# Forward attention segments in two head halves, with the token rows projected beside the memory rows

## The chip, the cores and the metric

One NeuronCore of one Trainium2 chip runs the whole program in one launch. The metric is device time in microseconds, the median of several executions. A single execution of each kernel is also recorded by the hardware profiler; the views of the profile quoted here come from that execution.

## The reference, cut to what matters

The function is a transformer block, forward and all its gradients. A sequence of 2048 rows of 448 is normalised, sent through a recurrent attention, added to the input, normalised again and sent through a gated FFN (1792 wide), and added once more. The recurrence is what sets the order of the work:

```python
for s in range(n_seg):                       # 64 segments of 32 rows
    h = concatenate([mem, xs], axis=1)       # 8 memory rows + 32 rows = 40
    q, k, v = h @ Wq, h @ Wk, h @ Wv         # 16 heads of 256
    scores = where(mask, q @ k.T * scale, -1e9)
    o = (softmax(scores) @ v) @ Wo
    mem = o[:, :M]                           # the next segment needs these 8 rows
    outs.append(o[:, M:])
```

The outputs are the block's result and the gradients of the input, the first memory and the seven weights, ten arrays in all.

## The kernel before, in words

The program has four stages: `forward_chain`, `ffn_phase` (FFN forward and backward), `backward_chain` and `tail_phase` (weight gradients from what the other stages stored). A tile is 128 rows, four segments; there are 16 tiles. A block is 16 segments.

**One forward segment.** The 40 rows of a segment stand as columns of `hT_roll`, the 32 rows first and the 8 memory rows after them. Heads are held in pairs (g = 0 on partitions 0 to 39, g = 1 on partitions 64 to 103). The steps, in order: `wpass` for Q and for K (L427, 128 matmuls of 40 columns each, evicted by DVE at L75 or ACT at L76); the scores of all heads into one PSUM tile (L486); the value rows, four PSUM tiles of two 512-column halves each (L494); the softmax on DVE and ACT over 128x320 (scale and mask L500, maximum L504, subtract L505, exp L506, sum L510, reciprocal L512, product L513); P turned by matmuls with the identity (L517) and copied into `PT_bd`, one half by DVE and one by ACT; the heads' outputs (L525); their memory columns copied to `o8`, which L535 multiplies with Wo: 32 matmuls of 8 rows, spread over four groups of 32 partitions of `pO`. The four groups are summed by copying them to fp32 (`om`, L541 and L542) and multiplying with a stack of four identities (L545), which also turns the result, and L548 casts that into `hT_roll` for the next segment. The 32 token columns of each head output go to `xblk`, and after every fourth segment L564 multiplies the whole tile with Wo (32 matmuls of 448 columns into `fx`); DVE adds the input rows (L565), the sum goes to `Hh` in memory, and its statistics are taken (L568, L569).

**Order.** Within `k.prio.crit()` instructions have a priority of their own, so they keep their order and stand ahead of everything else; what lies outside, such as L564, is put by the scheduler into places where TensorE would wait. Each engine then runs its own list strictly in order. SyncE (SP) issues the hardware queue's transfers and all transposing ones, GpSimd (POOL) the software queue's; both lists are in order too, and an issue waits there for its data. PSUM tiles for the chain come from one ring of five.

**Stores.** Every segment stores Q and P (POOL, L551 and L553) and K and V (SP, L552 and L554), and copies its memory rows on POOL (L555, L556). At the end of a tile `xblk` is turned by transposing DMA (L437) and stored to `X_o` (L439); at the end of a block `mblk`, the memory rows of the 16 segments, too. Weights are turned piece by piece through the same two staging buffers (L463, L464).

**FFN and tail.** In the last segment `_FFNLoads.at` asks for the FFN's weights at four places. The FFN needs the standard deviation of every tile: two square roots on ACT (L658), for tiles 0 to 11 and for the rest. `backward_chain` ends with the layer norm's gradient of tile 0: `DH` is fetched in two halves through one buffer (L983), and the result stored (L987). `tail_phase` begins with the gradient of Wo: `X_o`, 16 tiles of tokens and 4 of memory rows, is loaded on SP (L1031); the matching rows of `DHb` are loaded into `DCt` by four transfers on POOL (L1059); and L1095 sums over the 20 blocks, tokens first, six PSUM tiles at a time, 0.187 us a matmul.

Of the kernel before, what the change touches and what calls it, by code (L numbers as in the profile page):

```python
# [15 lines left out]
P = 128  # L16
# [129 lines left out]
def run_all(k: _K):  # L146
# [43 lines left out]
    nc.gpsimd.affine_select(out=mask1[:], in_=mask1[:], compare_op=ALU.is_ge, fill=-1e9,  # L190
# [13 lines left out]
    def dt(name, shape, dtype=BF16):  # L204
# [8 lines left out]
              X_o=dt("X_o", [NB, P, MC * P]), HC=dt("HC", [NB * P, DP]))  # L213
# [93 lines left out]
def forward_chain(k: _K):  # L307
# [13 lines left out]
    Wo_sb = W(96, MC, D)  # L321
    qT_b = [A(4 * i, 32, 64) for i in range(2)]
# [9 lines left out]
    mh = B(7.25, KC, P)  # L332
    PT_bd = B(0.25, 8, 2, L)
    o8_b = [B(1.5 + 0.5 * i, 32, M) for i in range(2)]
    x2_b = [B(2.5 + 0.875 * i, D) for i in range(2)]
    P_b = [B(4.25 + 0.625 * i, 8, L) for i in range(2)]
    h_b = [B(5.5 + 0.875 * i, D) for i in range(2)]
# [7 lines left out]
    om = k.f32("f1", DP, "om")  # L345
    nc.gpsimd.memset(om[:], 0.0)
    pO = k.po1()
    nc.vector.memset(pO[:], 0.0)

# [70 lines left out]
    def wpass(W_sb, s, dst):  # L420
        sl = s % NWIN
        pss = [k.ps1() for _ in range(3)]
        for j in range(MC):
            c = cj(j)
            b, jj = divmod(j, 12)
            for kc in range(KC):
                nc.tensor.matmul(pss[b][:, jj * L:(jj + 1) * L], lhsT=W_sb[:, kc, c * P:(c + 1) * P], rhs=hT_roll[:, kc, sl, :],  # L427
                                 start=(kc == 0), stop=(kc == KC - 1))
        for b in range(3):
            n = min(12, MC - 12 * b)  # L430
            k.evac(dst[:, 12 * b:12 * b + n, 0:L], pss[b][:, 0:n * L].rearrange("p (c n) -> p c n", n=L), "vsv"[b])
# [33 lines left out]

    for s in range(NSEG):
# [3 lines left out]
        qT, kT, Vs, o8, P_sb = qT_b[s % 2], kT_b[s % 2], V_b[s % 2], o8_b[s % 2], P_b[s % 2]  # L470
        xblk, x_t2, h_t = xblk_b[t % 2], x2_b[t % 2], h_b[t % 2]
        if r == 0:
            nc.gpsimd.dma_start(out=x_t2, in_=X2[t * P:(t + 1) * P, :])
        with k.prio.crit():
            wpass(Wq_sb, s, qT)
            if s == NSEG - 1:
                k.fl.at(0)
            wpass(Wk_sb, s, kT)
            if s == NSEG - 1:
                k.fl.at(1)  # L480
            pS = k.ps1()
            for h in range(8):
                for g in range(2):
                    for dc in range(DC):
                        j = 2 * (2 * h + dc) + g
                        nc.tensor.matmul(pS[64 * g:64 * g + 64, h * L:(h + 1) * L], lhsT=qT[:, j, :], rhs=kT[:, j, 0:L],  # L486
                                         start=(dc == 0), stop=(dc == DC - 1), skip_group_check=True)

            pV = [k.ps1() for _ in range(4)]
            for b in range(4):  # L490
                for kc in range(KC):
                    for g in range(2):
                        n = 4 * g + b
                        nc.tensor.matmul(pV[b][64 * g:64 * g + 64, 0:512], lhsT=hT_flat[:, kc, sl * L:sl * L + 64],  # L494
                                         rhs=Wv_sb[:, kc, n * 512:(n + 1) * 512],
                                         start=(kc == 0), stop=(kc == KC - 1), skip_group_check=True)
            if s == NSEG - 1:
                k.fl.at(2)
            S_sb = k.f32("f2", 8 * L, "S_sb")[:].rearrange("p (h n) -> p h n", n=L)
            nc.vector.scalar_tensor_tensor(  # L500
                out=S_sb, in0=pS[:, 0:8 * L].rearrange("p (h n) -> p h n", n=L), scalar=k.scale,
                in1=maskb[:].unsqueeze(1).to_broadcast([P, 8, L]), op0=ALU.mult, op1=ALU.add)
            mx = smal.tile([P, 8], FP32, name="mx")
            nc.vector.tensor_reduce(out=mx[:], in_=S_sb, axis=AX.X, op=ALU.max)  # L504
            nc.vector.tensor_tensor(out=S_sb, in0=S_sb, in1=mx[:].unsqueeze(2).to_broadcast([P, 8, L]), op=ALU.subtract)  # L505
            nc.scalar.activation(out=S_sb, in_=S_sb, func=ACT.Exp)  # L506
            for b in range(4):
                k.evac(Vs[:, b * 512:(b + 1) * 512], pV[b][:, 0:512], "s")
            ssum = smal.tile([P, 8], FP32, name="ssum")
            nc.vector.tensor_reduce(out=ssum[:], in_=S_sb, axis=AX.X, op=ALU.add)  # L510
            rs = smal.tile([P, 8], FP32, name="rs")
            nc.vector.reciprocal(out=rs[:], in_=ssum[:])  # L512
            nc.vector.tensor_tensor(out=P_sb, in0=S_sb, in1=rs[:].unsqueeze(2).to_broadcast([P, 8, L]), op=ALU.mult)  # L513
            pPT = k.ps1()
            for h in range(8):
                for g in range(2):
                    nc.tensor.matmul(pPT[64 * g:64 * g + L, h * L:(h + 1) * L], lhsT=P_sb[:, h, :],  # L517
                                     rhs=ident[:, 64 * g:64 * g + L], start=True, stop=True, skip_group_check=True)
            for g in range(2):
                k.evac(PT_bd[64 * g:64 * g + L, :, g, :],  # L520
                       pPT[64 * g:64 * g + L, 0:8 * L].rearrange("p (h n) -> p h n", n=L), "vs"[g])
            pso = [k.ps1() for _ in range(3)]
            for cl in range(16):
                b, i = divmod(cl, 6)
                nc.tensor.matmul(pso[b][:, i * 2 * L:(i + 1) * 2 * L], lhsT=Vs[:, cl * P:(cl + 1) * P],  # L525
                                 rhs=PT_bd[:, cl // 2, :, :].rearrange("p g n -> p (g n)"), start=True, stop=True)
            ov = []
            for b in range(3):
                n = min(12, 32 - 12 * b)
                v = pso[b][:, 0:n * L].rearrange("p (c n) -> p c n", n=L)  # L530
                ov.append((12 * b, n, v))
                k.evac(o8[:, 12 * b:12 * b + n, :], v[:, :, SEG:L], "vsv"[b])
            if s + 1 < NSEG:
                for j in range(MC):
                    nc.tensor.matmul(pO[32 * (j % 4):32 * (j % 4) + M, 0:D], lhsT=o8[:, j, :], rhs=Wo_sb[:, cj(j), :],  # L535
                                     start=(j < 4), stop=(j >= MC - 4), skip_group_check=True)
            for (c0, n, v) in ov:
                k.last_x = getattr(k, "last_x", {})
                k.last_x["svs"[c0 // 12]] = k.evac(xblk[:, c0:c0 + n, r * SEG:(r + 1) * SEG], v[:, :, 0:SEG], "svs"[c0 // 12])
# [9 lines left out]
        if s == 0:  # L549
            stats(2, NT, to_h.ins)  # L550
# [31 lines left out]
def ffn_phase(k: _K, back):  # L582
# [73 lines left out]
    for t0, t1_ in ((0, NT - 4), (NT - 4, NT)):  # L656
        with tc.issue_after(k.last_x["s"].ins):
            nc.scalar.activation(out=sd[:, t0:t1_], in_=mv2[:, t0:t1_, 1], func=ACT.Sqrt, bias=k.eps_t[:], scale=1.0)  # L658
        with tc.issue_after(k.last_x["v"].ins):
            nc.vector.reciprocal(out=rstd2[:, t0:t1_], in_=sd[:, t0:t1_])  # L660
# [552 lines left out]
```

## Time and profile before

| | us |
|---|---|
| median of 4 runs | 3345.87 |
| lowest and highest | 3337.11, 3356.5 |
| the profiled execution, time | 3337.11 |
| the profiled execution, span | 3335.3 |
| TensorE busy | 3035.5 (91%) |
| DVE busy | 1310.8 (39%) |
| ACT busy | 974.2 (29%) |
| POOL busy | 645.3 (19%) |
| mean granted TensorE clock | 0.972 |

The span runs from the first to the last instruction of the profiled execution; 1.8 us of its time lie around it. PE in the views is TensorE; PEld is its weight loading, which runs beside the matmuls. In the chain of waits a line is a start, a length and what was at work: it follows the end of the program back from instruction to instruction to whatever released each one. In a line of a group, the numbers behind the bar are busy time in us, the mean of one instruction in ns (for a matmul it includes the time in which the next ones already stream, so it is longer than the distance between two), and the idle time just before, with what ended it.

### The profile page before, as it was taken

What the parts mean: (1) busy time and instruction counts of PE and PEld (TensorE: products, weight loads), DVE (VectorE), ACT (ScalarE), POOL (GpSimd) and SP (SyncE); (2) the same over time, 40 slices, a digit from 0 to 9 for tenths busy, and PEclk for the clock granted to TensorE, in tenths of its full rate; (3) what the DMA queues carried; (4) which work ended last, traced back from release to release, by engine and by line L of the source; (5) the groups of instructions that cost most, each with busy time, mean ns of one, the idle gap of its engine ahead of it and who ended that gap; (6) DMA issues with size and microseconds to landing.
All of it is one profiled execution on the core that took longest, in us unless ns stands there. A gap on an engine that the chain in (4) does not pass through costs nothing.

```text
span 3335.3 us, 121108 instructions
## 1 busy us (share of the span) xinstructions
PE 3035.5 (91%) x55076; PEld 2054.6 (62%) x55086; DVE 1310.8 (39%) x2919; ACT 974.2 (29%) x2178; POOL 645.3 (19%) x1344
## 2 busy tenths in 40 slices
PE   5899999999999969995998999999999899999998
PEld 3676777777777746663666666666666544444443
DVE  4434444444344347773444444444454301111110
ACT  2323323333233223332333333333333201120110
POOL 3111211111111121221121111222222212112111
PEclk8999999999999989997999999999999999999999
DMA  7756865656675498888777788887878997969952
GB/s 262 196 152 168 214 180 162 188 162 182 183 197 162 135 288 192 202 197 274 151 167 167 156 168 163 169 167 165 174 166 174 271 277 209 198 177 198 198 148 70
DMA packets 993208, 619.57 MB, mean 186 GB/s; under 512 B 897476, under 2 KB 907796, under 8 KB 990196
## 3 DMA queue, kind: packets, MB, share of 16 engines
q1 hardware_dynamic: 921428, 361.57, 52.1%
q0 software_dynamic: 71264, 250.24, 22.1%
q8 instruction: 431, 7.06, 0.9%
q14 instruction: 85, 0.70, 0.1%
HBM read 123.54 MB, written 269.69 MB: 118 GB/s over the span
## 4 chain that ended last, share of the span: by engine, by line
PE 70%; DVE 9%; issue 9%; DMA 7%; ACT 2%; POOL 1%; SPq 1%; ACTq 0%; DVEq 0%; POOLq 0%
PE psf L427 12%; PE psf L1074 8%; PE po L903 7%; PE psf L494 5%; PE psf L860 5%; PE psf L837 4%; PE po L535 3%; PE psf L1095 3%; PE fx L564 3%; PE fx L962 3%; PE fx L731 2%; PE psf L650 2%; PE fx L1079 2%; DVE arA L75 2%; PE psf L925 2%
## 5 line engine op out<-in xcount | busy, mean ns | idle before, releaser
L76 ACT CAST arA<-psf 128x320 bf16<-128x320 f32 (+4 forms) x1139 | 487.3, 447 | 1537.2 <-PE psf L427 450.7
L75 DVE CAST arA<-psf 128x384 bf16<-128x384 f32 (+6 forms) x1029 | 492.5, 496 | 1014.5 <-PE psf L427 330.1
L427 PE MATMUL psf<-arA,arW 128*128 128x40 bf16 x16384 | 436.7, 181 | 38.6 <-issue 18.1
L427 PEld LDWEIGHTS <-arW 128*128 128x128 bf16 x16384 | 433.2, 97 | 55.2 <-issue 33.3
L903 PE MATMUL po<-arW,arA 128*32 128x448 bf16 x6144 | 358.5, 364 | 48.2 <-DVE arA L75 44.3
L494 PE MATMUL psf<-arW,arA 128*64 128x512 bf16 x2048 | 260.6, 383 | 3.6 <-DMA arW<-in_A_Wv_dram 3.6
L1074 PE MATMUL psf<-arW,arA 128*128 128x512 bf16 x1030 | 259.5, 379 | 0.0
L903 PEld LDWEIGHTS <-arA 128*32 128x32 bf16 x6144 | 154.8, 98 | 166.6 <-DVE arA L75 47.3
L1074 PEld LDWEIGHTS <-arA 128*128 128x128 bf16 x1440 | 136.0, 98 | 164.8 <-issue 13.8
L860 PEld LDWEIGHTS <-arW 128*128 128x128 bf16 x8192 | 213.0, 96 | 29.5 <-issue 29.5
L860 PE MATMUL psf<-arA,arW 128*128 128x40 bf16 x8192 | 217.0, 179 | 10.3 <-DVE arA L929 5.1
L650 PE MATMUL psf<-arW 128*128 128x256 bf16 x1344 | 156.4, 276 | 40.9 <-DMA arW<-arW 29.6
L494 PEld LDWEIGHTS <-arA 128*64 128x64 bf16 x2048 | 147.8, 111 | 71.1 <-DMA arW<-in_A_Wv_dram 4.6
L650 PEld LDWEIGHTS <-arW 128*128 128x128 bf16 x1344 | 132.9, 99 | 66.6 <-issue 33.7
L75 DVE CAST arB<-psf 40x320 bf16<-40x320 f32 x320 | 107.9, 337 | 99.9 <-PE psf L525 66.1
L837 PEld LDWEIGHTS <-arW 128*128 128x128 bf16 x2048 | 88.0, 101 | 67.9 <-issue 64.9
L76 ACT CAST arB<-psf 128x96 bf16<-128x96 f32 (+1 forms) x320 | 98.1, 307 | 105.4 <-DVE arB L75 52.8
L564 PE MATMUL fx<-arW,arA 128*128 128x448 bf16 x512 | 124.5, 353 | 0.6 <-ACT arA L76 0.6
L870 ACT COPY arA<-psf 128x1024 bf16<-128x1024 bf16 x128 | 123.3, 1015 | 5.9 <-PE psf L869 4.4
L535 PE MATMUL po<-arW,arB 128*8 128x448 bf16 x2016 | 110.7, 363 | 9.6 <-DMA arW<-in_A_Wo_dram 5.9
L837 PE MATMUL psf<-arB,arW 128*128 128x80 bf16 x2048 | 98.9, 203 | 18.9 <-DVE arB L887 7.1
L1095 PEld LDWEIGHTS <-arW 128*128 128x128 bf16 x606 | 58.9, 99 | 72.5 <-DMA arW<-X_o 13.0
(259 smaller groups left out, 3808.5 us busy)
## 6 DMA issues: line engine op xcount, KB each, us to landing
QT<-arA POOLq DMA_DIRECT2D x64, 512.0 KB, 4.9
KT<-arA SPq DMA_DIRECT2D x64, 512.0 KB, 3.6
VG<-arA SPq DMA_DIRECT2D x64, 512.0 KB, 3.8
X_o<-arA POOLq DMA_DIRECT2D x40, 512.0 KB, 4.4
X_v<-arA POOLq DMA_DIRECT2D x32, 512.0 KB, 6.7
X_k<-arA POOLq DMA_DIRECT2D x32, 512.0 KB, 4.0
X_q<-arA POOLq DMA_DIRECT2D x32, 512.0 KB, 4.2
arW<-X_o SPq DMA_DIRECT2D x30, 512.0 KB, 11.5
```

What stands on the lines that cost most here:

```text
L75: return nc.vector.tensor_copy(out=out, in_=in_)
L76: return nc.scalar.copy(out=out, in_=in_)
L427: nc.tensor.matmul(pss[b][:, jj * L:(jj + 1) * L], lhsT=W_sb[:, kc, c * P:(c + 1) * P], rhs=hT_roll[:, kc, sl, :], start=(kc == 0), stop=( ...
L494: nc.tensor.matmul(pV[b][64 * g:64 * g + 64, 0:512], lhsT=hT_flat[:, kc, sl * L:sl * L + 64], rhs=Wv_sb[:, kc, n * 512:(n + 1) * 512], sta ...
L535: nc.tensor.matmul(pO[32 * (j % 4):32 * (j % 4) + M, 0:D], lhsT=o8[:, j, :], rhs=Wo_sb[:, cj(j), :], start=(j < 4), stop=(j >= MC - 4), sk ...
L564: nc.tensor.matmul(px[:, 0:D], lhsT=xblk[:, j, :], rhs=Wo_sb[:, cj(j), :], start=(j == 0), stop=(j == MC - 1))
L650: nc.tensor.matmul(ps[:, f2 * 256:(f2 + 1) * 256], lhsT=Wt[:, kc, c * P:(c + 1) * P], rhs=xT[:, kc, :], start=(kc == 0), stop=(kc == KC - 1))
L837: nc.tensor.matmul(ps[b][:, i * 2 * L:(i + 1) * 2 * L], lhsT=lhs[:, cl, :], rhs=rhs_bd[:, cl // 2, :, :].rearrange("p g n -> p (g n)"), st ...
L860: nc.tensor.matmul(pss[b][:, jj * L:(jj + 1) * L], lhsT=WoT_sb[:, kc, c * P:(c + 1) * P], rhs=do_roll[:, kc, sl, :], start=(kc == 0), stop ...
L903: nc.tensor.matmul(pH[32 * (j % 4):32 * (j % 4) + 32, 0:D], lhsT=blk[nm][:, j, r * SEG:(r + 1) * SEG], rhs=WT[:, cj(j), :], start=(nm == " ...
L1074: nc.tensor.matmul(pa[2 * kc + g][:, 0:w], lhsT=lhs_of(b)[:, kc * P:(kc + 1) * P], rhs=rhs_of(b, g), start=(b == 0), stop=(b == nblk - 1), ...
L1095: nc.tensor.matmul(pa[i][:, 0:D], lhsT=lhs_of(b, i), rhs=rhs_of(b), start=(bi == 0), stop=(bi == len(nblk) - 1))
```

## The change

In the forward chain the 16 heads of a segment are handled in two halves of 8 (four pairs). Q, K, scores, softmax, transposes and head outputs are made for half 0 and half 1, in an order written out by hand, with the four value tiles and the projection between them:

```diff
+            wpass(Wq_sb, s, qT, 0, "vs")
+            wpass(Wk_sb, s, kT, 0, "sv")
+            wpass(Wq_sb, s, qT, 1, "vs")
+            pS0 = scores(0)
+            softmax(0, pS0)
+            wpass(Wk_sb, s, kT, 1, "sv")
+            value_rows(0)
+            pS1 = scores(1)
+            softmax(1, pS1)
+            value_rows(1)
+            transposed_p(0)
+            value_rows(2)
+            values(0)
+            transposed_p(1)
+            value_rows(3)
+            out_proj(0, 8)
+            values(1)
+            out_proj(8, MC)
```

The mask is no longer added by DVE. A matmul of the identity with the mask (`maskt`, 160 columns, filled with -1e9 over the scale) opens the sum of each score tile, and the scale moves into the exp:

```diff
+                nc.tensor.matmul(pS[:, 0:HB * L], lhsT=ident[:, :], rhs=maskt, start=True, stop=False, skip_group_check=True)
...
+                nc.vector.tensor_reduce(out=mx[:], in_=pS3, axis=AX.X, op=ALU.max)
+                nc.vector.tensor_tensor(out=Sx, in0=pS3, in1=mx[:].unsqueeze(2).to_broadcast([P, HB, L]), op=ALU.subtract)
+                nc.scalar.activation(out=Sx, in_=Sx, func=ACT.Exp, scale=k.scale)
```

Which columns go where changes as well. `xblk` now takes the columns M to L of each head output: 24 token rows and the 8 memory rows. `orr` (three buffers, in place of the two of `o8`) takes the first 8 token rows, and goes to `mblk`. So one projection per segment gives 24 token rows beside the memory rows, in two column halves of 256 and 192; the two sums are added by ACT and DVE, and two bf16 transposes and one cast give the next segment's memory:

```diff
+            def out_proj(j0, j1):
+                for j in range(j0, j1):
+                    jh = j % 2
+                    for dh in range(2):
+                        w = 256 if dh == 0 else D - 256
+                        q = 2 * jh + dh
+                        nc.tensor.matmul(pO[32 * q:32 * q + 32, 0:w], lhsT=xblk[:, j, r * SEG:(r + 1) * SEG],
+                                         rhs=Wo_sb[:, cj(j), 256 * dh:256 * dh + w],
+                                         start=(j < 2), stop=(j >= MC - 2), skip_group_check=True)
...
+            to_s = nc.scalar.copy(out=om[0:64, :], in_=pO[64:P, 0:256])
+            to_v = nc.vector.tensor_tensor(out=om2[0:64, :], in0=pO[0:64, 0:256], in1=om[0:64, :], op=ALU.add)
...
+                for c in range(2):
+                    nc.tensor.transpose(pm[:, 64 * c:64 * c + 64], om2[0:64, c * P:(c + 1) * P], ident[0:64, 0:64])
+        nc.gpsimd.dma_start(out=oh[s, M:SEG, 0:256], in_=om2[0:24, :])
+        nc.gpsimd.dma_start(out=oh[s, M:SEG, 256:D], in_=om2[32:56, 0:D - 256])
```

The product of a whole tile with Wo goes. In its place, once per block, `mblk` (the 8 token rows of each of 16 segments) is multiplied with Wo and stored beside the others in `Oh`, a new array in memory. From then on the block's four tiles are due: two segments after its fetch from `Oh`, at every third segment, a tile's residual is added and its statistics taken. The last four tiles are fetched and added within the first three steps of the FFN, and the square root for these tiles moves to the FFN's fifth step:

```diff
+        if due and jm % 3 == 1:
+            fetch(due[0], h_b[due[0] % 2], x2_b[due[0] % 2])
...
+        if due and jm % 3 == 0 and jm > 0:
+            n = due.pop(0)
+            residual(n, h_b[n % 2], x2_b[n % 2], to_v)
...
+        if n == last - 3:
+            rstd(NT - 4, NT)
...
+        if 0 < n < 3:
+            for t in (NT - 4, NT - 3) if n == 1 else (NT - 2, NT - 1):
+                k.late_residual(t, to_v)
+        if n < 2:
+            for t in (NT - 4, NT - 3) if n == 0 else (NT - 2, NT - 1):
+                k.late_fetch(t)
```

Since the rows of `X_o` are now mixed in this way, the tail loads `DCt` in the same mixture, by twenty transfers in place of four, and sums over the blocks in another order:

```diff
-    for t0, t1 in ((0, 4), (4, NT), (NT + 1, NB), (NT, NT + 1)):
-        nc.gpsimd.dma_start(out=DCt[:, t0:t1], in_=dcs[:, t0:t1])
-    order = list(range(NT)) + list(range(NT + 1, NB)) + [NT]
+    for g in range(NG):
+        nc.gpsimd.dma_start(out=DCt[:, NT + g], in_=dc8[g, :, 0:M])
+    for t0, t1 in ((NT // 2, NT), (0, NT // 2)):
+        for r in range(4):
+            nc.gpsimd.dma_start(out=DCt[32 * r:32 * r + 24, t0:t1], in_=dcx[r, M:SEG, t0:t1])
+            nc.gpsimd.dma_start(out=DCt[32 * r + 24:32 * r + 32, t0:t1], in_=dcm[r, :, t0:t1])
+    order = list(range(NT, NB)) + list(range(NT - 1, -1, -1))
```

## The prediction

> **What bounds the kernel now.** I read the busy table by 100 us first. It cuts the 3335.3 us span into forward (to about 1162), FFN (to about 1540), backward (to about 2650) and the closing weight gradients (to the end); TensorE is busy over 90% in nearly every cut, so the question is where it still waits. The row of the cast L548, which ends each forward segment, gives 63 starts from 56.9 to 1162.0: 62 segments in 1105.1 us, 17.82 us each. The change rewrites exactly these. Then I read one segment in the chain of waits (columns: start us, length us, what).
>
> ```profile
> 438.06 6.55 PE psf L427 x256
> ...
> 445.48 3.51 PE psf L494 x31
> ...
> 448.99 0.40 PE psf L517 x16
> ...
> 449.41 0.49 DVE arB L75
> ...
> 449.98 0.43 ACT arB L76
> ...
> 450.45 0.39 PE psf L525 x6
> ...
> 450.94 0.27 DVE arB L75
> ...
> 451.25 1.72 PE po L535 x32
> ...
> 452.99 0.40 DVE om L541
> ...
> 453.44 0.39 PE psf L545 x2
> ...
> 453.87 0.85 PE psf L545 x6
> ...
> 454.74 0.20 DVE arA L548
> ```
>
> From L548's cast at 437.82 to the next at 454.74 it is 16.92 us, without filler work. See two things. The softmax is not in it: the transposes L517 start the moment the value rows L494 end. What TensorE waits for comes after: 1.06 us for the two copies behind L517, 0.41 for the first memory copy, 0.48 for `om`, 0.27 for the last cast, 2.2 us in all. And L545, eight fp32 products that only sum and turn eight rows, holds the chain for 1.24 us.
>
> The second costly thing is the token product of each tile:
>
> ```profile
> L564 PE MATMUL fx<-arW,arA 128*128 128x448 bf16 x512 | 124.5, 353 | 0.6 <-ACT arA L76 0.6
> L535 PE MATMUL po<-arW,arB 128*8 128x448 bf16 x2016 | 110.7, 363 | 9.6 <-DMA arW<-in_A_Wo_dram 5.9
> ```
>
> L564 is filler, put into those waits; it lengthens the one or two segments that take it up. The four casts from 874.79 to 927.28 are 17.00, 17.23 and 18.26 apart, against 16.92.
>
> Last I read the start of the closing stage, in the chain and in the timeline of POOL (start, length, instruction, idle time and its releaser):
>
> ```profile
> 2655.07 11.29 DMA arW<-X_o
> ...
> 2666.42 21.46 DMA arW<-X_o
> ```
> ```profile
> 2650.86 0.55 POOL L983 DMA_DIRECT2D arB<-DH  x1 [0.61 <-DMA M_v<-arA]
> ...
> 2666.17 0.55 POOL L983 DMA_DIRECT2D arB<-DH  x1 [2.58 <-DVE arB L260]
> ...
> 2682.17 0.56 POOL L987 DMA_DIRECT2D out_dram<-arB  x1 [13.95 <-DVE arB L260]
> ```
>
> TensorE is fed here by transfers until 2690 and full from then on: what is lost before 2690 goes through to the end.
>
> **Forward, TensorE's work per segment, after.** Q and K, cut in halves but the same 256 matmuls: 6.55. Scores, 32 matmuls: 0.75. Two mask products of 160 columns: a 448-column matmul follows the last by 0.187 us (L564, 0.54 for two against 0.35 for one), so 0.07 each, 0.14. Value rows 3.51, transposes of P 0.40. Heads, 16 of 80 columns: 0.56 (0.73 less the 0.17 in which the last one drains). Output projection: 64 matmuls, 32 rows wide, four side by side, 256 and 192 columns; a group of four takes as long as its 256 columns, 0.107, and 16 groups 1.71 (L535 now: 1.55 plus the drain). Two bf16 transposes 0.05. Sum **13.67**; now it is 6.55+0.75+3.51+0.40+0.56+1.55+1.24 = 14.56.
>
> **Waits, after.** The copies of P for half 0 run beside value rows 2 (0.88), those for half 1 beside value rows 3 and the first quarter of the projection. I laid the ACT and DVE queues out by hand with widths scaled from rows: 320 elements 0.49 on DVE and 0.43 on ACT, 512 on ACT 0.58. A half softmax takes 2.15 (four DVE operations at 0.32, exp 0.36, reciprocal 0.20, hand-overs 0.3). Half 0 has 3.8 of TensorE work over it; half 1 has value rows 1 and 2, half of the transposes and half of the heads, 2.2: just covered, and if the cover fails by the length of one ACT eviction it costs 0.58. I count 0.2 before scores 1, 0.2 before heads 0, 0.1 before heads 1, 0.1 before the last quarter: 0.6; bounds 0 and 1.5. The end of the segment is drain 0.18, ACT copy 0.38, DVE sum 0.42, transposes 0.2, cast 0.20, hand-overs 0.2: 1.55. Sum 13.67+0.6+1.55 = **15.8** against 16.92: 1.1 each, times 62 = **69 us less** (bounds of the waits: 106 to 13).
>
> **Filler.** Twelve of the sixteen token products go; the excess above is 1.65 per tile in that run. Some of it is clock: **15 us less**. What I cannot see is the backlog. In the chain from 398.9 to 431.5 a segment waits on transposes (SP) and stores (POOL) at the end of a block of 16; the segment that ends at 437.82 takes 19.20, 2.3 too long. After, POOL gets two more stores per segment (0.54 each) and fetches for the residual, and the same 32 us of transfers must fit beside segments 1.1 shorter. Bounds: nothing, and 10 per block, 40. I take **15 more**, near two segments' shortening per block and the queue time of the extra stores. Residual add and statistics (about 1.4 of DVE per tile) move off L564 and go behind the segment's cast; DVE is idle over half of a segment.
>
> **FFN.** Its start waits for the store of the last K. In the new order the first rows are asked for before the weights, but the gate weights 3 us later than now: between 5 less and 5 more, 0. Inside: four late residuals, 1.4 of DVE each, and one more pair of table loads (1.28 each at L658 and L688) in ACT, which waits often: 0 to 10, I take **3**, the two loads.
>
> **Closing stage.** The four loads of DCt (L1059) become twenty, and the order of the issue on POOL matters. In the changed kernel's order the second half load of DH and the store of out_1 stand before five of the eight loads that make up tiles 8 to 15. Both wait on DVE: in the rows above the first leaves at 2666.17, the second at 2682.17. So the last piece for tile 15 leaves at about 2684.5 and lands 5 to 9 later (loads there take 9 to 14, and 6.7 once X_o is in): 2691. TensorE has done blocks 16 to 19 by then and waits; 16 tiles of six matmuls at 0.187 follow, 18, and eleven matmuls of the next group are put in between, so no loss: 2691+18-2 = 2707 against 2690: **16 more**; bounds 3 (loads land in 3, the DH halves faster) and 28 (each 13 late).
> The granted clock falls when TensorE starves here: 0.67 from 2670 to 2680. [...]
>
> **Sum.** -69-15+15+0+3+16 = -50. The profiled execution took 3337.1 (span 3335.3), so 3287; the median of the four runs is 8.8 above it, so **3296**.
>
> **Rivals.**
> 1. The projection is slower (slower than before). If each of the 64 matmuls needs what each of the 32 needs now, 0.047, the projection takes 3.0 and not 1.71: 1.3 per segment on the path, 81 in all: **3377**. It ends level at 0.8 per segment, 0.040 a matmul. For it: nothing in the trace has this shape at this rate. Against: L517 issues 16 narrow ones in 0.38, L427 one per 0.0256, and L903, as wide as the new one with 448 columns, takes 1.70 for 32, so it is columns that count. 7%.
> 2. Evictions become the bound. ACT's 5.48 per segment grow to about 6.9, nearly all of the growth in the second half, in strict order. At 0.7 per segment more: 43, **3339**. Against: each copy has a TensorE piece over it. 13%.
> 3. The closing stall isn't there (DH lands early, or the pieces do): **3280**. 12%.
> 4. The backlog at block ends takes 10 per block rather than 4: **3321**. 10%.
> 5. The change does nothing to the chain, since the softmax was hidden already and only the waits trade places: then only the filler and the tail remain, 3346-15+15+3+16 = **3365**. 3%.
> Forecast 55%.
>
> Half a per cent, 17 us, is about what a measurement here tells from no change. Below 3329: forecast, rivals 3 and 4 and a little of 2, **0.80**; within, most of 2, **0.10**; above 3363, rivals 1 and 5, **0.10**. Range: 3245 (waits 0, no backlog) to 3345 (waits near 1.5), which leaves rivals 1 and 5 out.
>
> **What would show it.** Cast to cast 15.8 in the quiet segments; the 64 projections of a segment in about 1.7; TensorE's wait before heads 0 below 0.3; the end chain 1.6 without fp32 products; a DMA wait on DHb near the start of the closing stage of 15 to 25 us. Wrong: quiet segments above 16.5, or a first closing group that ends as early as now.

## The result, and the profile after

The changed kernel takes 3367.27 us (median of 40 runs, 3345.76 to 3381.51) against 3352.3 for the kernel before (66 runs): a ratio of 1.0040, 95% interval 1.0029 to 1.0051. It is slower by 0.4%, inside the half per cent called no change; the forecast was 3296, outside its range of 3245 to 3345. The profiled execution of before (span 3335.3) is one of its quicker ones, that of after (3377.5) one of its slower ones. So the stages below add up to 42 us, of which about 15 are there in the medians, and a stage of a single profile carries some of that difference: the same forward code takes 1088.6 to 1101.3 us in the profiles of four kernels below (after, e1, e2, t1), and the backward stage, changed little or not at all, 1125.6 to 1153.6 in the 19 kernels. The mean granted clock belongs to a kernel more than to a run: over all runs 0.968 before (0.964 to 0.973), 0.958 after (0.953 to 0.963).

| stage of the profiled execution, us | before | after | predicted change |
|---|---|---|---|
| forward, first to last segment cast | 1105.1 | 1094.0 | -69 |
| last cast to first backward matmul (last segment and FFN) | 354.8 | 369.9 | +3 |
| backward, to the first closing matmul | 1136.4 | 1143.2 | 0 |
| closing: two halves of the gradient of Wo | 136.1 | 167.2 | +16 |

One quiet segment of the kernel after, in the chain of waits (start, length, what), from the cast at 452.55 to the one at 468.66:

```profile
452.55 0.18 DVE arA L597
...
452.77 4.96 PE psf L432 x192
457.73 0.07 PE psf L500
457.80 0.36 PE psf L505 x16
458.17 1.70 PE psf L432 x64
459.87 0.98 PE psf L527 x8
460.85 0.18 PE psf L500
461.03 0.39 PE psf L505 x16
...
463.33 0.45 PE psf L548 x8
...
463.99 1.00 PE psf L527 x8
464.99 0.55 PE po L561 x13
465.54 0.45 PE psf L548 x8
465.99 1.45 PE po L561 x35
...
467.52 0.38 ACT om L589
...
467.92 0.43 DVE arB L590
...
468.66 0.19 DVE arA L597
```

The segment has the predicted form: TensorE waits less than 0.1 us for evictions, the fp32 products are gone, and the end is one copy, one sum, two transposes and a cast. It takes 16.11, not 15.8, against 16.92. So the change does what it says, where nothing disturbs it. But the mean segment is 17.65, and the sum of what segments take above their quickest grew from 57 us to 95. The waits of TensorE in the forward (line waiting, who released it; us in total, times, longest) show where. After, 57 to 1150:

```profile
PE psf L596 <- DVE arB L590: 48.9, 49, 1.6
PE psf L432 <- issue: 36.8, 27, 2.8
PE psf L432 <- DVE arA L597: 13.0, 49, 0.3
PE psf L432 <- DVE arA L75: 12.9, 3, 4.6
```

Before, 57 to 1162:

```profile
PE psf L525 <- ACT arB L76: 34.7, 32, 1.1
PE psf L427 <- issue: 16.7, 26, 2.2
PE psf L486 <- issue: 9.5, 7, 2.1
```

The first and third lines of after are the end of each segment, which was planned. A line with "issue" is TensorE waiting for nothing that the profile shows. All such waits of the forward are 41.8 us, against 26.7 before; those of 1.2 us and more, which I count from here on, are 17 with 31.6 us, against 6 with 10.6. The fourth line is three waits of 4 to 5 us, one in each later block. The timelines of POOL, DVE and TensorE (start, length, instruction, idle time and its releaser) show the first:

```profile
392.11 0.57 POOL L623 DMA_DIRECT2D Oh<-arB  x1
...
397.90 0.55 POOL L483 DMA_DIRECT2D arB<-Oh  x1 [4.37 <-DMA Oh<-arB]
```
```profile
402.23 0.39 DVE L474 TENSOR_TENSOR arB<-arB 128x448 bf16<-128x448 bf16 x1 [6.86 <-DMA arB<-Oh]
```
```profile
403.73 1.23 PE L432 MATMUL psf<-arA,arW 128*128 128x40 bf16 x32 [4.03 <-DVE arA L75]
```

The block's memory rows reach `Oh` only after the token product of segment 15, which as filler lasts until segment 3 of the next block. The fetch of the first tile waits for that store, the residual L474 for the fetch, and it stands at the head of DVE's list in front of the evictions of Q and K. For the first tile of a block the two segments between fetch and residual are not enough.

The closing stage, as answer to the rows shown before (POOL; then TensorE; then a window of 18 us: the numbers after the stretch are its length and each engine's busy time, the last three the granted clock, the DMA share and GB/s):

```profile
2677.74 0.59 POOL L1052 DMA_DIRECT2D arB<-DH  x1 [11.31 <-DVE arB L260]
...
2684.70 0.60 POOL L1056 DMA_DIRECT2D out_dram<-arB  x1 [5.72 <-DVE arB L260]
...
2686.50 0.56 POOL L1134 DMA_DIRECT2D arW<-DHb  x1
```
```profile
2697.07 0.56 PE L1170 MATMUL fx<-arW 128*128 128x448 bf16 x1 [27.36 <-DMA arW<-X_o]
...
2713.96 0.55 PE L1170 MATMUL fx<-arW 128*128 128x448 bf16 x1 [2.82 <-DMA arW<-X_o]
...
2722.84 0.93 PE L1170 MATMUL fx<-arW,arA 128*128 128x448 bf16 x2 [2.21 <-DMA arA<-X_o]
```
```profile
2688.00:2706.00 18.00, 8.93 (x34) 4.10 (x35) 0.00 (x0) 0.00 (x0) 6.63 (x10) 0.60 1.05 223
```

The order on POOL is as predicted: DH's second half at 2677.7, `out_1` at 2684.7, the last pieces of DCt for tiles 8 to 15 behind them. The last of these is issued at 2686.5 and lands 9.1 later, at 2695.6. TensorE waits 38.2 us in six waits, where the kernel before waits 7.4: the difference, 30.8, is nearly the whole loss of the stage (31.1). Two things were not predicted. With the pieces in flight the 16 DMA engines have the same busy share as in the kernel before (1.05 against 1.03) and move 223 GB/s, where they moved 379 from 2670 to 2688. And the matmuls that wait are not those of the first group. Of the twenty products that the second half's sixth PSUM tile needs (`fx`), only eight run in their own place (2784.4 to 2792.4); twelve stand earlier in TensorE's list, one ahead of tile 15 and eleven ahead of tiles 7 to 0, and all six waits are theirs, for X_o tiles of the second half. The last pieces for tiles 0 to 7 are issued at 2695.9 and land at 2708.9, but these tiles are summed only from 2723.6 on.

### The profile page after: what moved, and what is told of

Read it like the earlier page. It is cut to its first block, busy times and chain, and to the rows that moved or that the text cites. A ratio compares the mean times of both kernels' runs of the same rounds, so it can differ in the third digit from the quotient of the medians.

```text
span 3377.5 us, 124932 instructions
## 1 busy us (share of the span) xinstructions
PE 2997.9 (89%) x56522; PEld 2022.5 (60%) x56532; DVE 1305.8 (39%) x3309; ACT 1034.7 (31%) x2501; POOL 726.8 (22%) x1507
## 3 DMA queue, kind: packets, MB, share of 16 engines
q8 instruction: 442, 7.24, 0.9%
## 4 chain that ended last, share of the span: by engine, by line
PE 68%; issue 10%; DVE 9%; DMA 7%; ACT 3%; POOL 1%; SPq 1%; ACTq 0%; POOLq 0%; DVEq 0%
PE psf L432 13%; PE psf L1149 8%; PE po L972 7%; PE psf L929 5%; PE psf L527 4%; PE psf L906 4%; PE po L561 4%; PE psf L1170 3%; PE fx L1031 3%; PE psf L710 2%; PE psf L994 2%; PE fx L1154 2%; DVE arA L75 2%; PE fx L800 2%; PE psf L548 2%
## 5 line engine op out<-in xcount | busy, mean ns | idle before, releaser
L76 ACT CAST arA<-psf 128x320 bf16<-128x320 f32 (+5 forms) x1267 | 518.2, 424 | 1500.5 <-PE psf L432 392.1
L75 DVE CAST arA<-psf 128x320 bf16<-128x320 f32 (+5 forms) x1093 | 488.9, 464 | 1024.3 <-PE psf L1149 262.5
L432 PE MATMUL psf<-arA,arW 128*128 128x40 bf16 x16384 | 450.5, 181 | 80.1 <-issue 38.2
L432 PEld LDWEIGHTS <-arW 128*128 128x128 bf16 x16384 | 439.6, 97 | 89.4 <-issue 66.9
L527 PE MATMUL psf<-arW,arA 128*64 128x512 bf16 x2048 | 276.4, 394 | 6.0 <-DMA arW<-in_A_Wv_dram 3.3
L972 PEld LDWEIGHTS <-arA 128*32 128x32 bf16 x6144 | 154.5, 98 | 168.6 <-DVE arA L75 44.1
L1149 PEld LDWEIGHTS <-arA 128*128 128x128 bf16 x1440 | 136.0, 98 | 164.8 <-issue 13.7
L929 PEld LDWEIGHTS <-arW 128*128 128x128 bf16 x8192 | 213.9, 96 | 28.9 <-issue 28.9
L929 PE MATMUL psf<-arA,arW 128*128 128x40 bf16 x8192 | 218.1, 180 | 10.8 <-issue 5.4
L710 PEld LDWEIGHTS <-arW 128*128 128x128 bf16 x1344 | 134.5, 100 | 73.4 <-issue 37.9
L527 PEld LDWEIGHTS <-arA 128*64 128x64 bf16 x2048 | 109.3, 113 | 65.9 <-issue 13.6
L561 PE MATMUL po<-arW,arA 128*32 128x256 bf16 (+1 forms) x4096 | 137.0, 263 | 6.0 <-DMA arW<-in_A_Wo_dram 5.2
L76 ACT CAST arB<-psf 40x160 bf16<-40x160 f32 (+3 forms) x448 | 120.8, 270 | 35.2 <-DVE arB L75 25.6
L906 PEld LDWEIGHTS <-arW 128*128 128x128 bf16 x2048 | 88.3, 101 | 67.6 <-issue 64.7
L561 PEld LDWEIGHTS <-arA 128*32 128x32 bf16 x4096 | 96.3, 97 | 40.6 <-DVE arB L75 19.3
L1170 PEld LDWEIGHTS <-arW 128*128 128x128 bf16 x606 | 60.0, 99 | 97.1 <-DMA arW<-X_o 35.2
L75 DVE CAST arB<-psf 40x160 bf16<-40x160 f32 (+3 forms) x384 | 108.5, 296 | 22.1 <-PE psf L536 22.1
```

Of the source, the lines that this page charges most:

```text
L75: return nc.vector.tensor_copy(out=out, in_=in_)
L76: return nc.scalar.copy(out=out, in_=in_)
L432: nc.tensor.matmul(ps[:, (j - j0) * L:(j - j0 + 1) * L], lhsT=W_sb[:, kc, c * P:(c + 1) * P], rhs=hT_roll[:, kc, sl, :], start=(kc == 0), ...
L527: nc.tensor.matmul(pV[64 * g:64 * g + 64, 0:512], lhsT=hT_flat[:, kc, sl * L:sl * L + 64], rhs=Wv_sb[:, kc, n * 512:(n + 1) * 512], start= ...
L561: nc.tensor.matmul(pO[32 * q:32 * q + 32, 0:w], lhsT=xblk[:, j, r * SEG:(r + 1) * SEG], rhs=Wo_sb[:, cj(j), 256 * dh:256 * dh + w], start= ...
L710: nc.tensor.matmul(ps[:, f2 * 256:(f2 + 1) * 256], lhsT=Wt[:, kc, c * P:(c + 1) * P], rhs=xT[:, kc, :], start=(kc == 0), stop=(kc == KC - 1))
```

## Theories and experiments

**T**: the pieces of DCt cost some 30 us in the closing stage. **R**: the residual of each block's first tile costs 12 us and more. **Q**: the waits on "issue" come from DMA traffic. **N**: the late residuals hold the FFN up. The rivals stand in the expectations. Ratios are to the kernel before in the same session; stage times are from one profiled execution each, the clock is the mean over the runs. e8 and x2 are the same kernel, measured in two sessions: 0.0020 apart in ratio, 6.8 us in the forward.

| kernel | ratio (95%) | clock | forward | closing |
|---|---|---|---|---|
| before | 1 | 0.968 | 1105.1 | 136.1 |
| after | 1.0040 (1.0029 to 1.0051) | 0.958 | 1094.0 | 167.2 |
| e1_dct_before | 0.9938 (0.9921 to 0.9954) | 0.963 | 1095.8 | 137.5 |
| e2_dct_act | 1.0042 (1.0024 to 1.0060) | 0.958 | 1088.6 | 164.6 |
| t1_whole_loads | 0.9937 (0.9913 to 0.9961) | 0.963 | 1101.3 | 139.0 |
| e3_res_late | 1.0004 (0.9983 to 1.0026) | 0.961 | 1069.0 | 167.6 |
| e4_no_late | 1.0038 (1.0024 to 1.0051) | 0.958 | 1095.6 | 172.8 |
| e6_plain_pieces | 1.0045 (1.0025 to 1.0064) | 0.957 | 1097.1 | 167.0 |
| e9_after_nostore | 0.9930 (0.9904 to 0.9956) | 0.962 | 1056.2 | 164.8 |
| e9b_before_nostore | 0.9943 (0.9924 to 0.9961) | 0.970 | 1093.5 | 137.7 |
| e9c_late_nostore | 0.9892 (0.9872 to 0.9911) | 0.965 | 1038.0 | 169.9 |
| e5_before_nopx | 1.0007 (0.9992 to 1.0022) | 0.958 | 1116.2 | 135.8 |
| e7_mixed_rows | 0.9894 (0.9863 to 0.9925) | 0.965 | 1081.1 | 138.2 |
| e8_mixed_last | 0.9908 (0.9874 to 0.9942) | 0.966 | 1074.9 | 139.5 |
| x2_mixed_base | 0.9888 (0.9861 to 0.9915) | 0.966 | 1081.7 | 138.6 |
| x1_mixed_nolate | 0.9873 (0.9847 to 0.9898) | 0.967 | 1065.8 | 140.1 |
| x3_mixed_split | 0.9860 (0.9835 to 0.9885) | 0.966 | 1056.1 | 138.2 |
| y1_split_filler | 0.9868 (0.9844 to 0.9892) | 0.974 | 1070.9 | 137.1 |
| y2_after_filler | 1.0102 (1.0083 to 1.0121) | 0.961 | 1109.5 | 167.8 |

### The closing stage

```diff
-    (the twenty loads of DCt, and the order NT..NB-1, NT-1..0)
+    (the four loads and the order of the kernel before)        # e1_dct_before
+    nc.scalar.dma_start(out=DCt[...]) for all twenty            # e2_dct_act
+    for t0, t1 in ((NT, NB), (12, NT), (4, 12), (0, 4)):        # t1_whole_loads
+        nc.gpsimd.dma_start(out=DCt[:, t0:t1], in_=dcs[:, t0:t1])   # order of after
```

> The changed kernel with the four transfers into DCt and the block order of the kernel before; the Wo gradient then pairs rows wrongly, the amount of work is the same. Theory T (the new DCt pieces starve TensorE at the start of the closing stage; in the profiles its first group ends 33 us later counted from the same point than before): 25 to 33 less than the changed kernel's 3367, so 3334 to 3342, and the first closing group ends about 37 us after its first matmul as in the kernel before. Rival F (the loss lies in the forward stage and the FFN, and the tail only moves its wait): 3360 or more.

> The changed kernel with the twenty DCt pieces issued by ACT's hardware queue and not by POOL. Theory T with order as the cause (pieces stand behind the DH half and the out_1 store on POOL): 15 to 25 less than 3367, so 3342 to 3352. Rival S (the pieces are slow as transfers, or share the bandwidth of the X_o loads, whoever issues them): 3360 to 3370, with the wait for tile 15 as long as now (27 us).

> The kernel after with four whole loads of DCt (128 partitions each) from the rows as they lie, but with the block order of the kernel after (rest rows first, then tile 15 down to 0). Leaves out: the gradient of Wo pairs rows that do not belong together. Theory P (the closing stage is late because of the sixteen loads of 24 and 8 partitions): a ratio to the kernel before of 0.992 to 0.996, as with the loads and the order of before together (0.9938), and no wait above 3 us for DCt or X_o in the first group. Rival O (the reversed order of the blocks is to blame): the ratio stays at 1.002 or above, and TensorE waits for X_o of the low tiles.

With four whole loads the closing part is back at 137.5 and 139.0, whatever the order of the blocks, and the ratio falls by 0.010, 34 us: T holds, a little above the 25 to 33 expected, and the reversed order is cleared. Issued by ACT the pieces cost as much as issued by POOL, so that they stand behind DH and `out_1` on POOL is not what decides. The wait only changes its place, as the waits of e2 from 2655 to 2735 show:

```profile
PE fx L1170 <- DMA arW<-X_o: 20.2, 7, 12.7
PE psf L1170 <- DVE arB L1003: 6.7, 1, 6.7
PE psf L1170 <- DMA arW<-DHb: 4.9, 1, 4.9
```

So the rival in e2's expectation has it (slow as transfers, whoever issues them), though the wait for tile 15 is 4.9 there and not 27. In t1 TensorE waits once for DCt and then 3.3 us for X_o:

```profile
2675.81 2.03 PE L1164 MATMUL psf<-arW,arA 128*128 128x448 bf16 x5 [7.93 <-DMA arW<-DHb]
```

t1 missed one number, no wait above 3 us: the first is 7.93. In the profiles of before, e1, t1 and e7, with whole loads, all twenty products of the second half run in their own place; in those of after, e2, e3, e4, e6 and y2, with the pieces, only 8 to 11 do. No run has the pieces without these products ahead, so how the 31 us divide between slow transfers and this order is not shown.

### The forward: residual, weight pieces, traffic

```diff
-        if due and jm % 3 == 1:                    # fetch at 1, 4, 7, 10; residual at 3, 6, 9, 12
+        if due and jm in (6, 8, 10, 12):           # e3_res_late; residual at 8, 10, 12, 14
-            nc.sync.dma_start_transpose(out=o3, in_=Ws[:, i0:i0 + n])
+            nc.sync.dma_start(out=o3, in_=...)     # e6_plain_pieces: plain copies, as many bytes
-        nc.sync.dma_start(out=dr["KT"][s], in_=...)
+        if s == 0:                                 # e9_after_, e9b_before_nostore: so for QT, KT, VG
+            nc.sync.dma_start(out=dr["KT"][s], in_=...)
```

> The changed kernel with fetch and residual of a block's tiles moved to its segments 6 and 8, 8 and 10, 10 and 12, 12 and 14 (from 1 and 3, 4 and 6, ...). Theory R (the first tile of a block is fetched before its rows of Oh have been written, so DVE stands still in the chain, three times 4 to 4.6 us of TensorE idle and a halved clock behind each): 12 to 22 less than 3367, so 3345 to 3355, and no wait of TensorE for L75 above 4 us. Rival C (the stalls only move to other segments): 3362 to 3370.

> The kernel after with the weight pieces of the forward fetched by plain copies of the same number of bytes instead of DMA transposes. Leaves out: the transposed weights, so the gradients that use them are wrong. Theory I (TensorE's long waits of 1.2 to 2.8 us that end on 'issue' come from the queues being full of transposes' small packets): the 'issue' waits of the forward above 1.2 us fall from 31.6 us to under 12, the lost clock of the forward from 41 to under 25 us, the forward gets 20 to 40 us shorter, ratio 0.992 to 0.998. Rival: the waits stay where they are (25 us or more) and the ratio stays at 1.002 to 1.006.

> The kernel after without the stores of qT, kT and Vs (512 KB each) in 63 of 64 segments; the backward pass reads the first segment's each time. Leaves out: the gradients that need the other segments' queries, keys and values are wrong. Theory Q (TensorE's long waits that end on 'issue' are its instruction packets, late behind busy DMA engines; each such wait has one packet of the instruction queue within 2 us): with DMA traffic of the forward more than halved, these waits above 1.2 us fall from 31.6 us to under 8, the lost clock with them, and the forward gets 20 to 50 us shorter. Rival B (these waits belong to the denser instruction stream itself, whatever the DMA does): 25 us or more of them stay, and the forward moves by less than 10 us.

> The same edit in the kernel before. Leaves out: the gradients that need the other segments' queries, keys and values are wrong. Theory Q: the kernel before had only 9 us of such waits, so it gains less than the kernel after, 5 to 25 us, and the difference of the two forwards grows from 11 us towards the 50 us that the quiet segments give. Rival B: both move alike, and the difference stays at 10 to 20 us.

> The kernel after without those stores and with the residuals late in each block. Leaves out: the gradients that need the other segments' queries, keys and values are wrong. If the forward's loss against the prediction is made of the instruction waits, the early residual and the clock that both pull down, the forward is now within 15 us of 63 quiet segments (62 x 16.1 = 1000 plus block ends), and 50 to 65 us below that of the kernel before without the stores. Rival: 30 us or more stay unexplained.

e3 takes 0.0036 off, 12 us, the least that R expected, and its three waits of 4 us are gone: R holds. In its profiled execution the forward is 25 us shorter and has half the lost clock (one less the granted clock, summed over 57 to 1125: 18.8 us, in the kernel after 39.3), but that execution, 3333.44, is one of the quickest of a kernel with a median of 3352.4; over all runs the clock rises from 0.958 to 0.961. e6 changes nothing: 34 us of "issue" waits remain, so the weights' transposes are not the cause, and my first form of Q falls.

Without the three large stores the "issue" waits of 1.2 us and more are 10.5 instead of 31.6 us (under 8 was expected; e1, e2 and t1, with the same forward as the kernel after, have 23 to 38), and the forward loses 38. The view of waits, for e9_after_nostore (57 to 1090):

```profile
PE psf L432 <- issue: 16.1, 16, 2.7
...
PE psf L432 <- DVE arA L75: 10.5, 3, 4.9
```

The forward of the kernel before gains only 12 from the same edit. So the difference of the two forwards grows from 11 to 37, and with the residuals late as well to 55 (1038.0 against 1093.5): near the 50 that 62 quiet segments give. Expected were 50 to 65. The profile of before is a quick one, so the ratios are the safer measure: the edit takes 0.0110 (37 us) off the kernel after and 0.0057 (19 us) off the kernel before, which is still twice as much. So the waits depend on the traffic. e9c still lies 39 above 62 times 16.11, where 15 and the block ends were expected; 21 of lost clock and 4.9 of "issue" waits are in that, and the rest is not explained. That what TensorE waits for are its instructions is argued, not shown: each of the 17 waits in the profile of after has one packet of the instruction queue q8 in it or in the 2 us before it, but one goes every 5.4 us anyway.

### The FFN

```diff
-                k.late_residual(t, to_v)     # and the fetches
+                pass                         # e4_no_late, x1_mixed_nolate
-        nc.gpsimd.tensor_copy(out=mblk[...], in_=orr)
+        if end: nc.vector.tensor_copy(out=mblk[...], in_=orr)    # e8: last segment only
+        else: nc.gpsimd.tensor_copy(out=mblk[...], in_=orr)
```

> The changed kernel without the four late residuals in the FFN: the last four tiles take the input rows alone as residual and statistics, early in the forward stage (this leaves the attention out of them). Theory N (late residuals cost the FFN two TensorE waits of 4 us for L756 and lengthen the transposes' waits; FFN 14 us longer in the profiles): 8 to 14 less than 3367, so 3353 to 3359. Rival: the FFN's extra time is its start (the last block's product stands ahead of the first transposes) and the second pair of table loads, which stay: 3364 to 3368.

> The version with late residuals and mixed rows, and in the last segment alone the copy of the memory rows on VectorE instead of POOL. Theory F (the FFN starts late since the last token product waits for POOL, which waits for a store): first gate matmul 4 to 8 us sooner after the last segment's evictions, ratio 0.001 to 0.002 below the version without this edit. Rival: the FFN's start is bound by the normalisation and its first loads, and nothing moves (within 1 us).

e4 comes to 1.0038 against 1.0040, as its rival says. e8 is built on e7 below. From the last cast to the first gate matmul are 23.1 us before, 27.8 after, and 23.6 in e8: theory F holds in the profile. The whole cannot tell it (0.9908 against 0.9894, intervals of 0.003).

> The version with late residuals in the blocks, mixed rows and the last memory copy on VectorE, and without the residuals of the last four tiles in the FFN. Leaves out: the last four tiles take x alone as their residual, fetched after the first block. Theory N (the late residuals hold up the FFN): ratio 0.002 to 0.004 below the same version with them (6 to 12 us), from the first gate matmul to the backward pass about 326 us instead of 334. Rival: the FFN's extra time in the profiles is the clock, the ratio stays within 0.0015.

> The version with late residuals in the blocks, mixed rows and the last memory copy on VectorE, as the base of the two others. From the earlier runs: ratio 0.988 to 0.993.

Without the late residuals two waits of TensorE for a DVE product (L756 in the kernel after), 7 to 8 us together in the runs with them, are gone. But the waits for DMA that follow are longer (27 us in x2, 36 in x1, first gate matmul to backward), and that stretch takes 335.6 in x1 and 333.7 in x2. It looks as if the transfers decide there and a wait that goes makes room for the next, but in e4 the stretch takes 326.3, so one profile each doesn't settle it. The ratios of x1 and x2 differ by 0.0015, less than their intervals. N falls as far as these runs can tell (about 8 us). Of the FFN's extra 15 us in the two profiles 5 are the start. The other 10 are at the edge of the spread: with the FFN of the kernel after that stretch takes 328.2 to 342.1 in fourteen profiles (342.1 is the kernel after itself), with the FFN of before 321.2 to 331.7 in three (331.7 is the kernel before). In the two the lost clock differs by 9 (25.7 against 17.1), at most 9 of the 10.

### Versions meant to beat both

```diff
+    DC=dt("DC", [NB * P, DP])                # e7: the mixed rows, as HC has them
+        if s == NSEG - 6:
+            nc.gpsimd.dma_start(out=dcr[:, 0:24, :], in_=dhr[:, 8:32, :])
+        if s == NSEG - 10:
+            nc.gpsimd.dma_start(out=dr["DC"][S:, :]..., in_=dhr[:, 0:8, :])
-            nc.gpsimd.dma_start(out=dr["DHb"][r0:r0 + P, :], in_=dhx...)
+            nc.gpsimd.dma_start(out=dcr[s:s + 16, 24:32, :], in_=dhx...)
```

> A correct version meant to beat both: the residual schedule moved late in each block (segments 6 to 14), and the mixed row order of the gradient written once in DRAM by two copies that lie under the backward pass, so that DCt comes by four whole loads. If the two measured costs of the kernel after (12 us for the early residual, 34 us for the pieces) add up: 3352 - 34 = 3318, ratio 0.988 to 0.992, forward excess as with the late residual alone, first closing group dense within 45 us of its first matmul. Rival: the DRAM copies disturb the backward pass by as much as they spare (ratio 0.995 to 1.0), to be seen as backward longer by over 10 us.

The residuals late, and the mixed rows written once in DRAM under the backward pass, so that DCt comes in four whole loads: 3317.54, ratio 0.9894. Backward takes 1138.9; the copies are hidden. In the same stage the DMA engines now move (window as above):

```profile
2660.00:2678.00 18.00, 13.36 (x59) 5.56 (x57) 0.88 (x2) 1.04 (x1) 1.00 (x2) 0.88 1.03 378
```

378 GB/s, at a busy share of 1.03 against the 1.05 above.

> The same version with the stores of qT, kT and Vs in halves, each issued when its half is evicted, so that the same bytes leave in smaller bursts over the segment. Theory of bursts: the waits on 'issue' above 1.2 us fall from about 30 us to under 18, forward 10 to 20 us shorter, ratio 0.003 to 0.006 below the base. Rival (the total of the traffic decides): waits within 6 us of the base's, ratio within 0.0015 of it.

```diff
     softmax(0, pS0)
+    nc.gpsimd.dma_start(out=dr["QT"][s][:, 0:1024], in_=qT[:, 0:16, :]...)   # x3; so for KT, VG
```

The same bytes in halves, each when it is ready: "issue" waits of 1.2 us and more fall from 35.9 to 14.7, the forward by 25.6 in the profiles, the median from 3317.83 to 3306.35. The profile of x2 is its slowest run; e7, e8 and x1, which store in the same bursts, have 24.9 to 33.5 us of these waits and forwards of 1065.8 to 1081.1, so x3 lies below all four, but by less than against x2. The ratio falls by 0.0028, just short of the 0.003 expected, and the intervals overlap. So the bursts matter for the waits, and not only the sum; what that is worth in time is 11 us in the medians and not settled. x3 has the lowest ratio of all versions: 1.4% below the kernel before.

### The filler

```diff
-                nc.tensor.matmul(px[:, 0:D], lhsT=xblk[:, j, :], ...)        # e5: in the kernel before
+        if r == 3 and jm < 15:                                             # y2 in after, y1 in x3
+            for j in range(MC):
+                nc.tensor.matmul(px[:, 0:D], lhsT=xblk[:, j, :], rhs=Wo_sb[:, cj(j), :], ...)
```

> The kernel before without the token product of a tile (32 matmuls on POOL's PSUM in every fourth segment); the residual takes other data of the same shape. Leaves out: the output of attention in the residual and all that follows from it is wrong. The prediction gave the 12 of 16 products that the change removes 15 us, so all 16 should be worth 20 (15 to 25 shorter forward). Rival: the products fill gaps of TensorE that stay open without them, and the forward gets 0 to 8 us shorter.

> The kernel after with the twelve removed token products put back as filler without use (32 matmuls of 448 columns in every fourth segment except the last of a block, 8 columns of the result copied). Theory K (the filler holds the granted clock up by filling TensorE's waits): the mean clock over the runs rises from 0.958 to 0.962 or more, and the time stays within 5 us of the kernel after or falls below it (ratio 1.000 to 1.0055). Rival (the filler only costs time): the clock stays at 0.958, and the time grows by 10 to 20 us (ratio 1.007 to 1.010).

> The same filler in the fastest version (late residuals in the blocks, mixed rows, stores in halves). Theory K: the clock rises from 0.966 to 0.968 or more and the time stays within 5 us (ratio 0.984 to 0.988). Rival: same clock, 10 to 20 us longer (ratio 0.989 to 0.992).

Without its 16 token products the kernel before is no faster: 1.0007. Two things take their place. TensorE's waits at three places that the products had filled grow from 48 to 117 us in the forward (L525, L545 and L427 for the cast), of which the first is

```profile
PE psf L525 <- ACT arB L76: 67.9, 62, 1.4
```

against 34.7 before. That leaves about 26 of the products' 96 us (512 matmuls at 0.187) as a gain, an estimate from these rows. And the granted clock falls from 0.968 to 0.958, about 31 us of the span (an estimate: difference times span); in the profiles the forward's lost clock is 56.3 against 23.8. The two are about as large. Put into x3 as filler, twelve products raise the clock from 0.966 to 0.974 (25 us) and cost nothing net; into the kernel after, they raise it only by 0.0026 (9 us) and cost 0.0062, 21 us. So in all three the clock moves the way theory K says, but how much it pays back differs: y1 went to K, y2 to the rival in time (0.9607 where 0.962 was expected). By these sums a product costs 1.8 to 2.5 us before the clock answers. Why the clock answers less in the kernel after stays open.

## Why the prediction was wrong, point by point

The step that failed is the one from the quiet segment to the whole forward. The prediction took what the disturbed segments cost above a quiet one to be unchanged (filler -15, backlog +15), and in the profiles this excess grew from 57 to 95 us. Beside it the closing stage cost twice what was forecast.

- **Quiet segments, -69.** Right in kind, a third too big: 16.11 instead of 15.8, -50. The projection took 2.0 in two parts, not 1.71; the heads 0.9, not 0.56, in two parts of 0.45; the mask 0.25, not 0.14; the waits came out smaller than the 0.6. Evictions were covered (rivals 1 and 2 fall: L561 did 64 matmuls in 2.0, not 3.0, and L548 waits for the copy of P less than 0.1). The end of the segment adds up to 1.58 in the prediction's own terms, not 1.55.
- **Filler, -15.** Wrong step: it counted TensorE's work and not the clock. e5 shows that taking the products away from the kernel before is worth nothing (1.0007), and that the clock falls, from 0.968 to 0.958, by about what they would have saved.
- **Backlog, +15.** Mis-sized and misplaced. Together with the filler the excess was to stay, and it grew by 39: 15 of "issue" waits, 13 of the first tile's residual, and the other 11 go with the lower clock (41.0 us of it lost in the forward against 23.8). I named the queue time of the new stores but took the two segments between fetch and residual as enough, and did not follow the first tile through the token product that it needs. The "issue" waits were in the profile before, 26.7 us, and I did not ask what a denser TensorE and the same traffic do to them. Rival 4, 10 per block, 40 in all, meets the 39 by luck: only 13 of it lie near the starts of the three later blocks.
- **FFN, +3.** The start, taken at 0, cost 5 (the last token product behind POOL; e8 gives it back); the late residuals cost nothing that a run shows, near the 3 taken for them.
- **Closing, +16.** The path was half right. The last piece for tile 15 was issued within 2 us of the forecast, 2686.5 against 2684.5, and landed 9.1 later, against 5 to 9: at 2695.6, not 2691. (The second half load of DH stands before four of the eight loads and `out_1` before three, not before five; and 2707 against 2690 is 17, not 16.) But the position on POOL is not what costs: e2 takes it away, and the stage still takes 164.6. What was missing is the rate, 223 against 379 GB/s, which made the X_o loads late, and the eleven matmuls "of the next group", which the sum took as free: they stand in TensorE's list ahead of tiles 7 to 0 and wait for X_o tiles of their own. It is 31 in the stage and 34 in the whole (e1). Rivals 3 and 5 fall with it and with the quiet segments; that rival 5's 3365 is near the measured 3367 is luck, since the chain did get shorter. My upper bound of 28 took each load as later, and none as slower.
- **Signs that were to show it wrong.** The quiet segment was below 16.5, and the closing group ended later: both steps held, and the sum did not. The signs watched the quiet case, while the loss was in the disturbed ones.

With the stage's own numbers the sum reads -50 + 39 + 15 + 7 (backward, the same code, within its spread) + 31 = +42, the difference of the two profiles. The medians differ by 15. The closing stage repeats (164.6 to 172.8 with the pieces, 135.8 to 140.1 without), so the 27 between belong to the other stages, and 39 and 15 are more likely too large than too small.

## What to carry to other kernels

A shorter quiet iteration is worth its shortening only if what was hidden in the old one still fits: list the transfers and the late inputs per block, and follow the first and the last iteration through them, not the middle one. If a large transfer has to be split, try it along time rather than along partitions: stores in halves over the segment took 10 to 21 us off the "issue" waits here (11 us in the medians, not settled), loads in pieces of 24 and 8 partitions lost 34. Matmuls put ahead as filler wait for their own inputs, in order (38.2 us in six waits in the closing stage): check that these land before the work behind them is ready. And before taking filler off an engine, look at the granted clock: it can be what the filler pays for (0.968 with the token products, 0.958 without them, e5).

## What the runs showed of the hardware

- Twenty loads of 24, 8 or 128 partitions and what ran beside them kept the DMA engines at a share of 1.05 with 223 GB/s (2688 to 2706, kernel after); with four whole loads of the same rows the engines moved 373 to 382 at 1.03 (t1 and e1 from 2670 to 2688, e7 from 2660 to 2678).
- TensorE waits 1.2 to 2.8 us for nothing visible: 31.6 us in a forward of 1094 with 179 GB/s of traffic, and 10.5 with 93 GB/s (e9). That these are waits for instructions is not shown. The instruction queue q8 carried 442 packets in the profile of after, 7.24 MB in all, 16 KB each, while TensorE ran 113,054 matmuls and weight loads; in that of before 431, while TensorE ran 110,162: 256 for each packet in both. What a packet holds is not shown.
- The mean granted clock over the runs of a kernel repeats: 0.9675 to 0.9677 for the kernel before in five sessions (single runs 0.964 to 0.973), 0.958 without its filler. In the kernel after, the clock was 0.50 from 214 to 216, behind two waits of 2.21 and 1.87 us, 3.5 us apart (they end at 208.3 and 213.7). It was 0.50 also around the end of each of the three waits for L75, of 4.03, 4.62 and 4.22 us (402 to 408, 685 to 691, 962 to 968). What lowers it is not shown.
